# A hybrid block on one Trainium2 core: a Silu on a column of ones as ScalarE's first instruction

## The chip, the core and the metric

The kernel runs on one core of a Trainium2 chip. A core has five engines with an instruction queue each: TensorE (PE; its weight loads are shown apart as PEld), VectorE (DVE), ScalarE (ACT), GpSimd (POOL) and SyncE (SP), which here only issues transfers. The metric is the device time of one launch in microseconds (us). The kernel before took 261.08 us, the median of three runs (260.71 to 262.23).

## The reference

Two blocks follow each other on a sequence of 2048 tokens with 640 channels, in bf16. The first is a convolution block of the H3 kind on a layer-normed input, the second a SwiGLU feed-forward block with 1728 inner columns:

```
h  = x + q' * (conv(kv, ssm_k) + kv * ssm_D)     q' = layernorm(x),  kv = shift_conv(k, 4 taps) * v
h2 = h + (silu(n @ w_gate) * (n @ w_up)) @ w_down     n = layernorm(h)
```

The long convolution is a causal one over all 2048 tokens, written in the reference with an FFT of length 4096.

## The kernel before

The sequence is cut into four blocks of 512 tokens, with 128 partitions of four tokens each. For each block the kernel makes `kv` (a four-tap convolution as small matmuls on transposed k, line 507), takes a short real transform of `kv` and of the filter by matmuls with a cosine and sine table (`WF`, line 317), multiplies spectra on VectorE (lines 552, 553, 578), transforms back (`WI`, line 747), gates and adds, normalizes again and transposes. The feed-forward part of block j runs while the convolution part of block j + 1 is worked on: gate and up products (line 835, and line 870 for the odd columns), Silu on ScalarE (line 852), the up product copied out of PSUM by ScalarE (line 859), their product on VectorE (lines 858 and 861), and the down product (line 902), which is added into the output.

Nothing is scheduled while the program runs or by a compiler. Each step is added with `plan.add` and gets a number in the order of adding; the table `ORDER` lists these numbers in the order in which the steps are emitted, and a negative number picks the step's other engine. A step is a function that may issue several instructions. Each engine works through its own instructions in that order and waits for others by semaphores. PSUM is four buffers `ps` of two banks; a product can only start when the buffer's last reader is done. Large operands share twelve SBUF buffers `big`.

[...] What this kernel asks of ScalarE is Copy (with and without a scale), Identity, Square and Silu. ScalarE's first step is an eviction of transposed k (line 488), a copy; the first Silu is that of line 852 in the feed-forward part of block 0, at some 51 us.

The step which the change touches is that of line 922. It is emitted among the first: a memset of the 128x128 tile `ident` by VectorE, which a select on GpSimd (line 923) then turns into the identity matrix, with which TensorE transposes k (line 486) and runs a few warming matmuls (line 936).

```
dve(100, lambda: nc.vector.memset(ap(ident), 1.0), [], [ident])
plan.add("pool", 700, lambda: nc.gpsimd.affine_select(ap(ident), ap(ident), ...), [], [ident])
```

Of the kernel before, what the change touches and what calls it, by code (L numbers as in the profile page):

```python
# [10 lines left out]
FP32 = mybir.dt.float32  # L11
BF16 = mybir.dt.bfloat16
I32 = mybir.dt.int32
ACT = mybir.ActivationFunctionType
# [5 lines left out]
P = 128  # L20
# [153 lines left out]
def kernel(ctx: ExitStack, tc: tile.TileContext, A_q, A_k, A_v, A_shift_k, A_ssm_k, A_ssm_D, B_x,  # L174
          B_w_gate, B_w_up, B_w_down, out):
    nc = tc.nc
# [23 lines left out]
    def fixed(shp, dt, name):  # L200
        return Buf(None, None, const.tile(shp, dt, name=name))

    def ap(b):
        if b.pool is None:
            return b.ap
        t = place[b.pool][b.at]
        _, how, sizes = views.get(b.kind, (None, None, None))
        return t.rearrange(how, **sizes) if how else t
# [15 lines left out]
    def dve(ns, fn, r, w):  # L224
        return plan.add("dve", ns, fn, r, w)
# [26 lines left out]
    ident = fixed([P, P], BF16, "ident")  # L252
# [666 lines left out]
                     [], [(o, k)])  # L919


    dve(100, lambda: nc.vector.memset(ap(ident), 1.0), [], [ident])
    plan.add("pool", 700, lambda: nc.gpsimd.affine_select(ap(ident), ap(ident), [[-1, P]], ALU.is_equal, 0.0, base=0, channel_multiplier=1), [], [ident])

    def blank():
# [127 lines left out]
```

## Time and profile before

| what | value |
| --- | --- |
| median of three runs | 261.08 us |
| lowest and highest | 260.71, 262.23 us |
| the profiled execution's own time | 260.93 us |
| its span, first to last instruction | 259.1 us |
| granted TensorE clock | 1.00 |
| TensorE, VectorE, ScalarE busy | 248.4, 206.6, 180.1 us |
| ScalarE table loads | 2, of 1283 ns each |

A profile line of a group reads: line of the code, engine, operation, what it writes and reads with the shape, number of instructions; then busy time in us and the mean of one in ns; then the engine's idle time just before them and which instruction ended it. A time line reads: start, length, engine, line, operation, operands, and in brackets the idle time before and its releaser. The chain is the sequence of work that ended last, followed back from the end of the program.

### The profile page before, as it was taken

Reading aid. Unit: us, or ns where it says so; the run is one execution under the profiler, and the core shown is the slowest. Engines: PE = TensorE matmul, PEld = TensorE weight load, DVE = VectorE, ACT = ScalarE, POOL = GpSimd, SP = SyncE. Lnnn points to the kernel's source line nnn. Section 1 sums busy time; section 2 is a strip of 40 time slices with the busy share of each in tenths; the row PEclk is TensorE's granted clock in tenths of the full one; section 3 lists DMA queues with packets and bytes.
Section 4 is the critical chain, followed back from the end, with each engine's and each line's share of the span. In section 5 each row is a group of like instructions: output and inputs, shape, how many; then the busy total and the mean of one; then the engine's idle time right before and its main releaser. Section 6 shows DMA issues by size and latency. Waiting matters only on the chain.

```text
span 259.1 us, 5062 instructions
## 1 busy us (share of the span) xinstructions
PE 248.4 (96%) x2012; PEld 145.1 (56%) x2027; DVE 206.6 (80%) x297; ACT 180.1 (69%) x308; POOL 16.6 (6%) x26
## 2 busy tenths in 40 slices
PE   6799988989999999999999999999999999999995
PEld 3566656444545677654445577544447764444663
DVE  1779999979999999999999999999999821121222
ACT  3399989998999999969969978742553662342300
POOL 2000000000000011020002201400001003000000
PEclk9999999999999999999999999999999999999999
DMA  6999997499569798699491415997699406000011
GB/s 195 353 147 307 272 160 193 106 242 274 111 206 310 129 266 184 118 203 273 123 215 25 78 51 97 220 285 211 176 245 242 100 3 76 0 3 0 0 53 51
DMA packets 73379, 40.82 MB, mean 158 GB/s; under 512 B 33606, under 2 KB 71180, under 8 KB 73356
## 3 DMA queue, kind: packets, MB, share of 16 engines
q1 hardware_dynamic: 71052, 37.88, 59.3%
q0 software_dynamic: 2304, 2.62, 7.0%
q8 instruction: 16, 0.26, 0.4%
q14 instruction: 7, 0.06, 0.1%
HBM read 30.01 MB, written 4.59 MB: 133 GB/s over the span
## 4 chain that ended last, share of the span: by engine, by line
PE 76%; DVE 9%; ACT 7%; DMA 4%; issue 2%; SPq 1%; DVEq 0%; ACTq 0%
PE ps L835 38%; PE ps L902 22%; PE ps L317 7%; PE ps L870 5%; DMA big<-in_A_q_dram 4%; PE ps L747 3%; DVE S L578 2%; ACT S L303 1%; DVE row L760 1%; DVE big L578 1%; DVE bn L677 1%; ACT big L535 1%; ACT big L303 1%; DVE S L352 1%; PE ps L507 1%
## 5 line engine op out<-in xcount | busy, mean ns | idle before, releaser
L835 PE MATMUL ps<-big,big 128*128 128x512 bf16 x469 | 105.3, 379 | 1.5 <-ACT sg L852 0.9
L835 PEld LDWEIGHTS <-big 128*128 128x128 bf16 x480 | 46.8, 98 | 56.2 <-issue 1.6
L902 PE MATMUL ps<-wd,tT 128*128 128x320 bf16 (+2 forms) x447 | 63.6, 299 | 0.4 <-ACT big L535 0.4
L902 PEld LDWEIGHTS <-tT 128*128 128x128 bf16 x448 | 43.2, 98 | 18.4 <-issue 0.4
L852 ACT ACTIVATE sg<-ps 128x1024 bf16<-128x1024 f32 (+1 forms) x28 | 27.0, 964 | 38.1 <-PE ps L835 18.6
L317 PE MATMUL ps<-big,WF 128*128 128x320 bf16 x240 | 39.3, 299 | 1.5 <-ACT S L303 0.5
L552 DVE TENSOR_TENSOR big<-S,S 128x2560 bf16<-128x2560 bf16 x24 | 35.1, 1485 | 0.1
L553 DVE TENSOR_TENSOR S<-S,big 128x2560 bf16<-128x2560 bf16 x24 | 34.9, 1485 | 0.0
L317 PEld LDWEIGHTS <-WF 128*128 128x128 bf16 x240 | 23.1, 97 | 14.0 <-issue 3.1
L861 DVE TENSOR_TENSOR tT<-sg,sg 128x1024 bf16<-128x1024 bf16 (+1 forms) x22 | 14.6, 664 | 13.1 <-ACT sg L859 13.1
L692 ACT ACTIVATE row<-big,sm 128x640 bf16<-128x640 bf16 x23 | 21.0, 928 | 2.7 <-DVE sm L643 2.7
L620 ACT ACTIVATE row<-big 128x640 bf16<-128x640 bf16 x28 | 20.7, 745 | 2.6 <-DVE big L771 2.1
L859 ACT CAST sg<-ps 128x1024 bf16<-128x1024 f32 (+1 forms) x22 | 21.4, 972 | 1.3 <-PE ps L835 1.2
L303 ACT CAST S<-ps 128x320 bf16<-128x320 f32 (+1 forms) x41 | 20.2, 553 | 2.5 <-PE ps L317 2.3
L908 POOL DMA_DIRECT2D out_dram<-row x12 | 10.7, 1052 | 105.2 <-ACT row L907 105.2
L303 ACT ACTIVATE big<-ps 128x640 bf16<-128x640 f32 (+1 forms) x27 | 16.3, 645 | 0.5 <-PE ps L317 0.3
L858 DVE TENSOR_TENSOR tT<-sg,ps 128x1024 bf16<-128x1024 bf16 (+1 forms) x6 | 6.3, 1042 | 13.1 <-PE ps L835 10.6
L747 PE MATMUL ps<-S,WI 128*128 128x320 bf16 x96 | 15.2, 299 | 0.2 <-DVE S L578 0.2
L663 ACT ACTIVATE row<-big 128x640 bf16<-128x640 bf16 x20 | 15.0, 759 | 0.2 <-DMA big<-row 0.2
L870 PE MATMUL ps<-big,big 128*128 128x512 bf16 x57 | 13.8, 379 | 0.1
L747 PEld LDWEIGHTS <-WI 128*128 128x128 bf16 x112 | 10.6, 98 | 5.8 <-issue 0.6
L578 DVE TENSOR_TENSOR big<-S,S 128x2560 bf16<-128x2560 bf16 (+1 forms) x10 | 12.2, 1222 | 0.1
(90 smaller groups left out, 231.5 us busy)
## 6 DMA issues: line engine op xcount, KB each, us to landing
big<-in_B_w_gate_dram SPq DMA_DIRECT2D x24, 320.0 KB, 5.0
big<-in_B_w_up_dram SPq DMA_DIRECT2D x24, 320.0 KB, 4.6
big<-in_A_v_dram SPq DMA_DIRECT2D x4, 640.0 KB, 5.8
big<-in_A_ssm_k_dram SPq DMA_DIRECT2D x4, 640.0 KB, 8.6
big<-in_A_q_dram SPq DMA_DIRECT2D x4, 640.0 KB, 5.8
wd<-in_B_w_down_dram SPq DMA_DIRECT2D x1, 2080.0 KB, 10.7
out_dram<-big SPq DMA_DIRECT2D x3, 640.0 KB, 5.1
out_dram<-row POOLq DMA_DIRECT2D x12, 160.0 KB, 5.0
```

What stands on the lines that cost most here:

```text
L303: (lambda: nc.scalar.activation(dst(), src(), ACT.Copy, scale=2.0)) if twice else (lambda: nc.scalar.copy(dst(), src())),
L317: nc.tensor.matmul(ap(ps)[:, h, 0:NH], w, ap(src)[:, r, h * NH:(h + 1) * NH], start=(first and i == 0), stop=(last and i == len(rs) - 1), ...
L552: dve(1490, lambda b=b, xs=xs, hs=hs: v.tensor_mul(flat2(b), X.part(xs), H.part(hs)), [X.at(xs), H.at(hs)], [b])
L553: dve(1490, lambda b=b, dst=dst, f=f: f(A.part(dst), A.part(dst), flat2(b)), [b], [A.at(dst)])
L620: act(930, lambda r=r, junk=junk: nc.scalar.activation(ap(junk), ap(x)[:, r, :], ACT.Square, scale=D ** -0.5, accum_out=sm(s, 1)[:, r:r + ...
L692: nc.scalar.activation(ap(row), ap(x)[:, r, :], ACT.Identity, bias=sm(s, 5)[:, r:r + 1], scale=sm(s, 4)[:, r:r + 1])
L747: nc.tensor.matmul(ap(ps)[:, w, 0:NH], m, src[:, w * NH:(w + 1) * NH], start=(i == 0), stop=(i == len(terms) - 1))
L835: nc.tensor.matmul(of(ps, i), ap(w)[:, k, off:off + P], ap(hT)[:, k, lo:lo + n], start=(k == 0), stop=(k == KT - 1))
L852: act(1010 if wide else 600, lambda: nc.scalar.activation(of(sg), of(*gate), ACT.Silu), [gate[0]] if gate[0] is up[0] else [(gate[0], gate ...
L859: op = plan.add("act", 1010 if wide else 590, lambda: nc.scalar.copy(of(co), of(*up)), psu + [sg], [co] + tt, ("dve", 1230 if wide else 69 ...
L870: nc.tensor.matmul(ap(ps)[:, i, :], ap(w)[:, k, off:off + P], ap(hT)[:, k, :], start=(k == 0), stop=(k == KT - 1))
L902: nc.tensor.matmul(ap(to)[:, hf, 0:n], ap(tT)[:, c, at:at + P], ap(wd)[:, c, d0:d0 + n], start=(c == order[0]), stop=(c == order[-1]))
```

## The change

The step of line 922 issues three instructions where it issued one: the memset of `ident`, a memset of a new tile `one` of 128 partitions and one column in fp32, and a Silu by ScalarE on that column, in place. Nothing reads `one` afterwards. Both new instructions lie in the same step, so the numbers of the steps and the table `ORDER` stay as they were.

```
-    dve(100, lambda: nc.vector.memset(ap(ident), 1.0), [], [ident])
+    one = fixed([P, 1], FP32, "one")
+
+    def first():
+        nc.vector.memset(ap(ident), 1.0)
+        nc.vector.memset(ap(one), 1.0)
+        nc.scalar.activation(ap(one), ap(one), ACT.Silu)
+    dve(100, first, [], [ident])
```

## The prediction

> **What bounds the kernel now.** I read the page's busy times first, then the ScalarE groups with shapes kept apart, then the chain that ended last around the second table load, then TensorE's waits, and last the time line of all engines around 50 us and of ScalarE and SyncE at the start. The page:
>
> ```profile
> span 259.1 us, 5062 instructions
> ...
> PE 248.4 (96%) x2012; PEld 145.1 (56%) x2027; DVE 206.6 (80%) x297; ACT 180.1 (69%) x308; POOL 16.6 (6%) x26
> ```
>
> TensorE is idle for 259.1 - 248.4 = 10.7 us of the span. That is the whole pot from which an edit that adds and removes no matmul can draw. The ScalarE groups hold two table loads, one at the head of the program and one under the line of the Silu:
>
> ```profile
> L488 ACT ACT_TABLE_LOAD x1 | 1.3, 1283 | 0.8 <-PEq L1037 0.8
> L852 ACT ACT_TABLE_LOAD x1 | 1.3, 1283 | 0.0
> ```
>
> The second stands on the chain that ended last (start, length, what):
>
> ```profile
> 49.34 0.72 ACT row L663 x2
> 50.07 1.28 ACT L852
> 51.36 1.03 ACT sg L852
> 52.40 0.04 issue
> 52.44 4.91 PE ps L835 x22
> ```
>
> ScalarE runs without a gap before it, so the load takes 1.28 us of a queue that is full, and the first Silu (51.36 to 52.38) frees the PSUM buffer that TensorE's next gate or up product needs. From 52 us on TensorE is followed nearly without a break, and its waits there are two:
>
> ```profile
> PE ps L835 <- ACT sg L852: 0.9, 1, 0.9
> PE ps L902 <- ACT big L535: 0.4, 1, 0.4
> ```
>
> The time line of all engines shows who else the load holds up:
>
> ```profile
> 47.71 3.83 PE L835 MATMUL ps<-big,big 128*128 128x512 bf16 x17
> ...
> 50.07 1.28 ACT L852 ACT_TABLE_LOAD   x1
> ...
> 52.44 5.77 PE L835 MATMUL ps<-big,big 128*128 128x512 bf16 x25 [0.90 <-ACT sg L852]
> ...
> 54.44 0.99 ACT L859 CAST sg<-ps 128x1024 bf16<-128x1024 f32 x1
> ...
> 55.47 0.69 DVE L861 TENSOR_TENSOR tT<-sg,sg 128x1024 bf16<-128x1024 bf16 x1 [1.39 <-ACT sg L859]
> ```
>
> TensorE loses 0.90 us and VectorE 1.39 us, both behind ScalarE. At the head of the kernel:
>
> ```profile
> 0.82 1.28 ACT L488 ACT_TABLE_LOAD   x1 [0.82 <-PEq L1037]
> ...
> 0.99 0.17 DVE L922 MEMSET ident<- 128x128 bf16 x1
> ...
> 1.99 0.29 POOL L923 TENSOR_SCALAR_AFFINE_SELECT ident<-ident 128x128 bf16<-128x128 bf16 x1
> ...
> 2.31 0.19 DVE L948 TENSOR_TENSOR eye<-ident 128x64 bf16<-128x64 bf16 x1 [1.16 <-POOL ident L923]
> ...
> 5.47 1.88 ACT L488 COPY kT<-ps 128x640 bf16<-128x640 bf16 x3 [3.37 <-PE ps L486]
> ```
>
> **The change, part by part.** *Removed: the second load.* After it, the copies, squares and Identity passes of lines 303, 620, 663, 692 and 859 go on to the end with no third load, so the set that holds Silu serves all that this kernel asks of ScalarE. If that set is loaded first, nothing calls for another: one load of 1.283 us is gone at 50.07.
>
> *Added on VectorE: a memset of 128 ones.* The nearest row is the memset of line 495, 0.07 us; that of line 922 with 128 columns took 0.17. I take 0.07. It stands at 1.16 us, where VectorE then waits 1.16 us for GpSimd, so it lies in that wait. GpSimd's select needs the memset of ident, done at 1.16, and starts at 1.99 behind GpSimd's own memset (1.39 + 0.52 = 1.91). Even if it waited for both memsets (1.23) nothing would move. Without that cover it would cost 0.07.
>
> *Added on ScalarE: a Silu of one column.* No row has this shape. From below: 0.206, the mean of the 128x1 accumulator reads of line 620. From above: 0.587, the shortest Silu of line 852 (512 columns). I take 0.25, nearer to the one column. The load ahead of it either starts at 0.82 as now, or waits for the memset and runs 1.25 to 2.53. So the Silu ends between 2.3 and 3.2 us. Queued behind it is the copy of line 488, which waits for TensorE until 5.47: 2.3 to 3.2 us of cover. Cost nothing; if the cover were gone, 0.25 plus the 0.4 by which the load may slide.
>
> *Moved: nothing else.* The three new instructions lie in one step of the order table, so the numbers of all steps stay; no DMA issue is passed or moved, on SyncE's queue or GpSimd's.
>
> *What the removed load is worth.* ScalarE gains 1.28 us from 50.07 on, if its next instructions have their inputs. The first Silu reads a gate product, the cast of line 859 at 54.44 the up product after it, whose last matmul ended at 50.48. Even a Silu that had to wait for that one would start at 50.53, 0.83 earlier than now. TensorE can't gain more than its own stall. By the waits it is 0.90. By matmul starts it is a little more: the last matmul before the stall ends at 51.54, and at 0.379 us each it began at 51.16; in an undisturbed stretch one starts every 0.216 us, so the next could have begun at 51.38 and not at 52.44: 1.06. VectorE's wait of 1.39 goes almost wholly (1.28). That matters, since VectorE has next to no idle time from there to 80 us (29.85 of 31.26 us busy between 52.44 and 83.70, the 1.39 being all the rest) and would otherwise hold TensorE at the old pace.
>
> *What is late next.* Transfers. SyncE's run of issues from 50.49 to 57.5 hangs on TensorE at 50.48, before the stall, and does not move. What it brings has room: a gate load issued at 50.88 landed at 55.87 and is first read by TensorE at 58.9; the x block landed at 54.75 and is first read at 58.66; the transposes landed at 59.08 and are read at 65.2. So the least room is 3.0 us, against a shift of 1. The tightest place is VectorE at 62.9, where it passes waits on transfers whose last landing was the output store's, 62.28, if it needs that one: with the store up to 0.14 earlier (it was released by VectorE's line 643 at 57.72, when SyncE had been ready since 57.55), VectorE would keep about 62.9 - 62.28 + 0.14 = 0.76, say 0.8, of its 1.28. The later issues (71.79 behind TensorE's line 317, and so on) move with the engines that release them.
>
> The sum: 0.8 if VectorE is held at 62.9, 1.06 if nothing holds; I take 0.9, the stall as the waits count it. Lower bound of the gain: nothing, if a later wait eats it. Upper bound: 1.06 plus the 0.38 of line 902 at 89.5, where ScalarE's evictions are late: 1.44. The profiled execution took 260.93 (span 259.1 and 1.8 around it) and becomes 260.0; it lies 0.15 under the median of the runs, 261.08, so against that median: 261.08 - 0.9 = 260.2. That is 0.34%, inside the 0.5% that a measurement of this kernel can tell from no change.
>
> **The rivals.** *The gain is given back (chance 0.19).* ScalarE, VectorE and TensorE are all within 2% of full between 84 and 112 us (ScalarE 21.92 of 22.48, VectorE 22.03, TensorE 22.48), and ScalarE's evictions release TensorE there within 0.05 us of need, so a transfer of that stretch that keeps its old time (DMA share 1.01 between 83.7 and 89.5) would hold all three. For it: no slack in any engine. Against it: those transfers are issued after waits on TensorE and ScalarE, and shift too. Time: 260.8 to 261.1.
>
> *More than the stall comes out (0.12).* VectorE and ScalarE get 1.28 where TensorE gets 1.06, so the small late evictions after 61 us and the 0.38 at 89.5 could go as well. Against it: ScalarE at 83.70 itself waits 0.25 for TensorE, so it can't arrive there with more than TensorE's shift. Time: 261.08 - 1.44 = 259.6, which is 0.55% faster.
>
> *Two loads remain (0.03).* If whatever places the loads put them otherwise, the Silu at the head would bring its set and the next copy another, and the load at 50.07 would stay. For it: now the first copy at the head did bring a set without Silu. Against it: a set that serves the next function is kept, as the long run after 51.36 with Silu and copies mixed shows. Time: 261.1, for the second load at the head still ends by 4.5 us, before 5.47. [...]
>
> *Slower: the transfers of 56 to 62 us collide (0.08).* With ScalarE and VectorE 1.28 earlier, the output store of 640 KB is not held any more by line 643 and goes out with the transposes, the k load and the gate load, in a stretch where the DMA share was already 1.68 (56 to 58 us). If that delays what TensorE reads next, the stall comes back larger. It decides only when a landing slips by more than 3.0 - 1.06 = 1.9 us; to be slower by 0.5% (1.3 us) it must slip by 1.9 + 1.06 + 1.3 = 4.3. Against it: the store moves by 0.14 at most. Time: 262.4 to 262.8 if it happens.
>
> **How the numbers follow.** The forecast has 0.58: 260.2, its own range 259.7 to 260.9. The runs of before spread from 260.71 to 262.23, so a median of a few runs can sit 0.3 to 0.5 off. The range for 8 in 10 goes from 259.4, which takes in the larger gain, to 261.5, which takes in the gain lost and an uneven run; left out are the collision and the tails. Faster by over 0.5% means under 259.77: the larger gain, 0.12, and about one in ten of the forecast's own spread, 0.06: 0.18. Slower by over 0.5% means over 262.4: the collision, 0.08. Same: 0.74.
>
> **What would show it.** In the profile after: one table load, with a Silu of 128x1 behind it before 3.3 us, and the copies of line 488 still at about 5.5; no load near 50 us and the first Silu of the gate at about 50.1; no wait of TensorE on it near 51.4; line 861's first product at about 54.2 and not 55.47; the rest of the time line 0.8 to 1.1 us earlier up to the end, with a span of 258.0 to 258.3. The prediction is wrong if TensorE's idle time after 52 us grows by what it lost at 52.4, above all at 62 to 90 us, or if a second load stands at 5 us.

## The result, and the profile after

The changed kernel took 259.81 us (median of 22 runs) where the kernel before, run beside it, took 261.02 (22 runs): a ratio of 0.9953 with a 95% interval of 0.9937 to 0.9968. That is 1.21 us less, where 0.9 was forecast, and the time lies inside the forecast's own range. By its interval the gain is 0.8 to 1.6 us, so the time alone does not tell 1.21 from 0.9; what is finer than that below rests on the traces. The profiled execution took 259.64 us with a span of 257.8 (before: 260.93 and 259.1). The page of the changed kernel:

```profile
span 257.8 us, 5063 instructions
...
PE 248.2 (96%) x2012; PEld 145.4 (56%) x2027; DVE 206.8 (80%) x298; ACT 178.7 (69%) x308; POOL 17.6 (7%) x26
```

TensorE is now idle for 257.8 - 248.2 = 9.6 us and not 10.7; ScalarE is busy for 1.4 us less, of which the load without the new Silu makes 1.28 - 0.20 = 1.08. Among ScalarE's groups with shapes kept apart there is one load where there were two, and the new Silu:

```profile
L927 ACT ACT_TABLE_LOAD x1 | 1.3, 1283 | 0.8 <-PEq L1043 0.8
L927 ACT ACTIVATE one<-one 128x1 f32<-128x1 f32 x1 | 0.2, 203 | 0.0
```

The time line of the start (start, length, what) shows where the new instructions lie:

```profile
0.82 1.28 ACT L927 ACT_TABLE_LOAD   x1 [0.82 <-PEq L1043]
...
1.10 0.06 DVE L926 MEMSET one<- 128x1 f32 x1
...
1.99 0.29 POOL L929 TENSOR_SCALAR_AFFINE_SELECT ident<-ident 128x128 bf16<-128x128 bf16 x1
2.11 0.20 ACT L927 ACTIVATE one<-one 128x1 f32<-128x1 f32 x1
2.31 0.19 DVE L954 TENSOR_TENSOR eye<-ident 128x64 bf16<-128x64 bf16 x1 [1.15 <-POOL ident L929]
...
5.64 0.69 ACT L488 COPY kT<-ps 128x640 bf16<-128x640 bf16 x1 [3.33 <-PE ps L486]
```

The load starts at 0.82 as before: it did not wait for the memset that its Silu waits for. GpSimd's select is still at 1.99. The memset lies in VectorE's wait for it, and the Silu ends at 2.31, 3.33 us before ScalarE's next instruction has its input. That this is at 5.64 and not at 5.47 is not the Silu's doing: among the runs below it is 5.64 without a Silu at the head (the second load in idle time) and 5.45 with it (the shorter delay). Around 50 us the time line of all engines now reads:

```profile
47.32 8.80 PE L835 MATMUL ps<-big,big 128*128 128x512 bf16 x40
...
49.65 0.22 ACT L663 ACTIVATION_READ_ACCUMULATOR row<-big 128x1 f32 x1
49.74 1.04 ACT L852 ACTIVATE sg<-ps 128x1024 bf16<-128x1024 f32 x1
...
52.81 1.03 ACT L859 CAST sg<-ps 128x1024 bf16<-128x1024 f32 x1
...
53.87 0.69 DVE L861 TENSOR_TENSOR tT<-sg,sg 128x1024 bf16<-128x1024 bf16 x1
```

The Silu follows line 663 without a load between, 1.62 us earlier than before (49.74 against 51.36), TensorE runs through, and line 861 has no wait any more. Of the 1.62, 0.17 was there ahead of this place already (see below); the other 1.45 is more than the load's 1.28. Now the Silu starts 0.09 us after the start of the accumulator read ahead of it and overlaps it (49.65 and 49.74). In the kernel before, that read lay here:

```profile
49.83 0.22 ACT L663 ACTIVATION_READ_ACCUMULATOR row<-big 128x1 f32 x1
```

and the load began only when it was over, at 50.07. So the load took some 1.45 us of a full queue and not 1.28. TensorE's waits on other engines from 49 us to the end are down to one:

```profile
PE ps L902 <- ACT big L535: 0.5, 1, 0.5
```

**Where the 1.3 us came from.** Pair the instructions of the two traces, engine by engine in their order, and take the difference of their starts: that gives a shift along the span. TensorE's is -0.17 at 43 to 51 us, -1.23 from the stall on, -1.34 from 61 us, -1.48 from 69 to 166 us, -1.39 from there and -1.28 from 184 us to the end. VectorE's and ScalarE's are -0.17 to -0.18 ahead of 50 us, some -1.6 at 55 us, -1.47 to -1.49 at 81 us and -1.28 at the end. So the step at 50 us is worth 1.31 us for all three engines, some 0.2 of it is given back late, and 0.17 was there ahead of the change's reach.

The 1.31 is more than TensorE's stall of 1.06. The other part is two stalls that no list of waits showed. TensorE's own time line, of the kernel before:

```profile
59.77 1.46 PE L835 MATMUL ps<-big,big 128*128 128x512 bf16 x6
61.19 0.70 PE L317 MATMUL ps<-big,WF 128*128 128x320 bf16 x4
...
67.67 1.79 PE L317 MATMUL ps<-big,WF 128*128 128x320 bf16 x12
69.44 1.24 PE L870 MATMUL ps<-big,big 128*128 128x512 bf16 x5
```

and the same place of the changed kernel:

```profile
58.76 1.24 PE L835 MATMUL ps<-big,big 128*128 128x512 bf16 x5
59.84 0.71 PE L317 MATMUL ps<-big,WF 128*128 128x320 bf16 x4
...
66.32 1.79 PE L317 MATMUL ps<-big,WF 128*128 128x320 bf16 x12
67.95 1.24 PE L870 MATMUL ps<-big,big 128*128 128x512 bf16 x5
```

Look at the starts alone. Twelve matmuls of line 317 and then line 870: 69.44 - 67.67 = 1.77 before, 67.95 - 66.32 = 1.63 after, 0.14 less for the same twelve. At 61.19 matmul by matmul: the last of line 835 starts at 60.85, and the next start is 0.334 us later where 0.216 is the pace, 0.12 too many. Neither line carries a bracket with idle time, because in the time line the end of a matmul lies behind the next start, so behind 512 columns a delay under about 0.16 us (0.379 - 0.216) leaves no gap, nor does one behind the 320 columns of line 317 (0.30 long, 0.136 apart). 1.06 + 0.12 + 0.14 = 1.32.

### The profile page after: what moved, and what is told of

Same layout as the page of the kernel before. It is cut to its first block, busy times and chain, and to the rows that moved or that the text cites. A ratio compares the mean times of both kernels' runs of the same rounds, so it can differ in the third digit from the quotient of the medians.

```text
span 257.8 us, 5063 instructions
## 1 busy us (share of the span) xinstructions
PE 248.2 (96%) x2012; PEld 145.4 (56%) x2027; DVE 206.8 (80%) x298; ACT 178.7 (69%) x308; POOL 17.6 (7%) x26
## 4 chain that ended last, share of the span: by engine, by line
PE 85%; DVE 7%; ACT 5%; issue 2%; POOL 0%; ACTq 0%; DVEq 0%; POOLq 0%
PE ps L835 40%; PE ps L902 23%; PE ps L317 10%; PE ps L870 5%; PE ps L747 3%; DVE S L578 2%; PE ps L507 1%; DVE big L578 1%; ACT S L303 1%; PE ps L942 1%; ACT big L535 1%; DVE big L537 1%; ACT big L303 1%; PE ps L793 1%; ACT row L620 1%
## 5 line engine op out<-in xcount | busy, mean ns | idle before, releaser
L317 PE MATMUL ps<-big,WF 128*128 128x320 bf16 x240 | 39.1, 299 | 1.6 <-ACT S L303 0.8
L317 PEld LDWEIGHTS <-WF 128*128 128x128 bf16 x240 | 23.2, 97 | 13.7 <-issue 3.1
L303 ACT CAST S<-ps 128x320 bf16<-128x320 f32 (+1 forms) x41 | 20.2, 554 | 2.3 <-PE ps L317 2.1
L303 ACT ACTIVATE big<-ps 128x640 bf16<-128x640 f32 (+1 forms) x27 | 16.3, 646 | 0.3
```

The source lines that it names most:

```text
L303: (lambda: nc.scalar.activation(dst(), src(), ACT.Copy, scale=2.0)) if twice else (lambda: nc.scalar.copy(dst(), src())),
L317: nc.tensor.matmul(ap(ps)[:, h, 0:NH], w, ap(src)[:, r, h * NH:(h + 1) * NH], start=(first and i == 0), stop=(last and i == len(rs) - 1), ...
```

## The experiments

"Step" below is the change of that shift between 43 to 50 us and 70 to 100 us, against the trace of the kernel before. It leaves out what differs at the head: there, at 43 us, the profiled executions of these kernels lie between 0.54 us early and 1.94 us late, whatever was edited.

**The same start with another function.** The only edit against the changed kernel is the function:

```
-        nc.scalar.activation(ap(one), ap(one), ACT.Silu)
+        nc.scalar.activation(ap(one), ap(one), ACT.Copy)
```

> The changed kernel with the Silu on the column of ones replaced by a Copy on it: the tile, the memset and ScalarE's extra instruction stay, but the first set loaded is again one without Silu, so the second load stands again ahead of the first gate Silu. Theory (the gain is the stall behind the second load and nothing else): two loads, TensorE waits 0.9 us at about 52.4 again, time that of the kernel before within 0.3 us, ratio 0.999 to 1.001. Rival A (the head of the kernel, the new tile's place in memory or the extra instruction gave part of the gain): 0.2 to 0.6 us faster than before, ratio 0.998 or less, with the stall in place.

Measured: 260.83 us, ratio 1.000 (0.9981 to 1.0019), step 0.00. Its time line around 50 us:

```profile
49.59 1.28 ACT L852 ACT_TABLE_LOAD   x1
50.88 1.02 ACT L852 ACTIVATE sg<-ps 128x1024 bf16<-128x1024 f32 x1
...
51.96 4.26 PE L835 MATMUL ps<-big,big 128*128 128x512 bf16 x19 [0.89 <-ACT sg L852]
```

The second load is back and with it the stall. The tile, the memset and one more instruction at the head are worth nothing by themselves: it is the function that counts.

**The same without the new tile.** The column is one of a tile that is written later anyway (`diag`):

```
-        nc.vector.memset(ap(one), 1.0)
-        nc.scalar.activation(ap(one), ap(one), ACT.Silu)
+        nc.vector.memset(ap(diag)[:, 0, 0:1], 1.0)
+        nc.scalar.activation(ap(diag)[:, 0, 0:1], ap(diag)[:, 0, 0:1], ACT.Silu)
```

> The changed kernel with the Silu on one column of the tile diag, which is written anew later, and no new tile, so that every tile lies in memory where it lay before. Theory: as the changed kernel, ratio to before 0.9953 within 0.0015 and one load. Rival A, memory part: less gain, ratio 0.997 to 1.000.

Measured: 259.45 us, ratio 0.9949 (0.9927 to 0.9972), step -1.31. The profiled execution has a long span, 259.8, since it was 1.94 us late at 43 us already; behind 50 us it gains as the others do. The place of the new tile plays no part.

**Both loads kept, the second one in idle time.** The Silu on the column stands ahead of ScalarE's first copy of line 399 instead of at the head:

```
-        nc.scalar.activation(ap(one), ap(one), ACT.Silu)          # at the head
...
+            def turned_out(copy, r=r, pt=pt):                     # the eviction at line 399
+                if early and copy == nc.scalar.copy:
+                    early.pop()
+                    nc.scalar.activation(ap(one), ap(one), ACT.Silu)
+                copy(ap(gT)[:, r, :], turned(pt)[:, 0:D])
...
```

> The Silu on the column of ones is not ScalarE's first instruction but stands just ahead of block 0's first copy of line 399, at about 8 us, where ScalarE idles for 3.5 to 3.9 us. Two loads, as in the kernel before, but the second hidden. Theory (what costs is where the load stands, not how many there are): as the changed kernel, ratio 0.9953 within 0.0015; the second load at about 7.5 us, copy of line 399 not later than before. Rival B (each load costs its 1.3 us, wherever it stands): as before, 0.999 to 1.001.

Measured: 259.54 us, ratio 0.9956 (0.9935 to 0.9977), step -1.31. ScalarE's time line:

```profile
7.54 1.28 ACT L404 ACT_TABLE_LOAD   x1
8.84 0.20 ACT L404 ACTIVATE one<-one 128x1 f32<-128x1 f32 x1
11.07 0.69 ACT L405 COPY big<-ps 128x640 bf16<-128x640 bf16 x1 [2.03 <-PE ps L399]
```

Two loads, and the whole gain. So the number of loads has no price here; what was paid for was the place of the second, in a queue without a gap.

**The changed kernel once more**, without an edit.

> The changed kernel unaltered, for a second profile on the same chip as the three above. Theory: ratio 0.9953 within 0.0015; TensorE's starts after 72 us 1.2 to 1.5 us earlier than in the first profile of before, and those up to 12 us shifted by whatever the first loads land late, in either direction, up to 0.5 us: the 0.17 us by which the first profile of after was early ahead of the stall is no part of the change. Rival A: the same 0.17 us early at 44 to 50 us again.

Measured: 259.66 us, ratio 0.9943 (0.9921 to 0.9966), step -1.31. At 43 us it lies 0.18 us later than the kernel before, where the first profile of the changed kernel lay 0.17 earlier. The head's 0.17 is therefore no part of the change's effect. It gives back 0.34 us between 150 and 184 us, more than the 0.19 of the first profile.

**Two more loads ahead of the first Silu.** An Exp on the column, at the place where the load had stood, brings a load, and the Silu behind it another (51.15 and 52.66 us in the trace of this run):

```
+            def silu(c=c, j=plan.block):
+                if j == 0 and c == 0:
+                    nc.scalar.activation(ap(one), ap(one), ACT.Exp)
+                nc.scalar.activation(of(sg), of(*gate), ACT.Silu)
...
```

> The changed kernel with an Exp on the column of ones just ahead of the first gate Silu of block 0, where the kernel before had its second load. Exp needs another set, so two loads of 1.28 us and an instruction of 0.2 us come in there: some 2.75 us. Theory as it now stands (ScalarE's queue is the bound from about 44 us to about 88 us, so its time there counts one for one): steps from 50 us on 2.7 to 2.8 us later than in the changed kernel, time about 262.4, ratio to before 1.0055. Rival C (only TensorE's own stall counts: it has about 0.4 us of slack there in the changed kernel and later waits soak up more): 2.0 to 2.35 later, ratio 1.003 to 1.004.

Measured: 263.74 us, ratio 1.0103 (1.0062 to 1.0145), step +2.92 against the kernel before, so 4.23 against the changed one. That is some 1.5 us more than the 2.75 which the loads and the Exp should take. TensorE's time line and the table of engines by stretches of 2 us (granted clock behind POOL) tell why:

```profile
55.03 7.24 PE L836 MATMUL ps<-big,big 128*128 128x512 bf16 x25 [2.39 <-ACT sg L856]
```

```profile
54.00:56.00 2.00, 0.97 (x4) 0.44 (x4) 1.17 (x1) 2.00 (x4) 0.00 (x0) 0.89 1.04 355
56.00:58.00 2.00, 2.00 (x6) 0.70 (x5) 0.00 (x0) 2.00 (x6) 0.00 (x0) 0.50 1.30 255
58.00:60.00 2.00, 2.00 (x9) 0.79 (x8) 1.94 (x3) 1.76 (x4) 0.00 (x0) 0.75 0.78 156
```

The stall itself is 2.55 us between matmul starts, 1.49 more than before. Behind it the granted clock fell to 0.50, and matmuls that start every 0.216 us began up to 0.427 apart from 55.46 to 59.09 us: 1.68 us more. The sum, 1.49 + 1.68, less the 0.26 of the two late stalls, which don't occur in this run, is 2.91. What the expectation had left out is that a stall can cost more than its length, as this one did by 1.68 us. The last runs below look for the length at which it does.

**Two more loads where ScalarE is idle.** The same Exp ahead of the sixth Silu of the last block (`j == NB - 1 and c == 4`), where ScalarE waits 4.68 us:

> The changed kernel with the same Exp and its two loads ahead of the sixth Silu of the last block, at about 232 us, where ScalarE idles for 4.7 us and waits for VectorE's line 858. Theory: 2.75 us fit into 4.7, that Silu still starts as soon as VectorE releases it, no change: ratio to before 0.9953 within 0.0015. Rival B (each load costs its time): 2.6 to 2.8 us slower than the changed kernel, ratio 1.005.

Measured: 260.66 us, ratio 0.9979 (0.9954 to 1.0004). This didn't go as expected:

```profile
233.51 1.28 ACT L855 ACT_TABLE_LOAD   x1
234.80 0.20 ACT L855 ACTIVATE one<-one 128x1 f32<-128x1 f32 x1
238.15 1.28 ACT L856 ACT_TABLE_LOAD   x1 [3.15 <-DVE tT L863]
239.44 1.02 ACT L856 ACTIVATE sg<-ps 128x1024 bf16<-128x1024 f32 x1
```

The first load went into the idle time; the second did not, though 3.15 us of it were left. It starts only when VectorE's line 863 has released the Silu behind it, so the Silu comes 1.3 us late. In this trace TensorE loses 0.17 us by it at 242 us and the end comes 0.18 later; the median lies 0.85 above that of the changed kernel, but the two intervals overlap, so what it costs in the time stays unclear.

**Both loads behind each other in that idle time.** With a Silu of the column behind the Exp, the second load belongs to an instruction that waits for nothing:

```
                 if j == NB - 1 and c == 4:
                     nc.scalar.activation(ap(one), ap(one), ACT.Exp)
+                    nc.scalar.activation(ap(one), ap(one), ACT.Silu)
```

> The changed kernel with two more table loads, both ahead of the sixth Silu of the last block and both behind each other without a wait of that Silu's between them: load, Exp of one column, load, Silu of one column, about 2 x 1.283 + 2 x 0.2 = 2.97 us, in an idle time of ScalarE of 4.7 us. Theory (a load costs only what stands behind it at that moment): the four end about 1.7 us before the Silu's input is there, the Silu and line 861 do not move, and the time is that of the changed kernel, ratio to before 0.995 within 0.0015. Rival (a load costs its 1.28 us wherever it stands, or each drains the engine for more): ratio 0.9995 to 1.005.

Measured: 259.69 us, ratio 0.9934 (0.9911 to 0.9958), step -1.31.

```profile
232.44 1.28 ACT L855 ACT_TABLE_LOAD   x1
233.74 0.20 ACT L855 ACTIVATE one<-one 128x1 f32<-128x1 f32 x1
233.96 1.28 ACT L856 ACT_TABLE_LOAD   x1
235.25 0.20 ACT L856 ACTIVATE one<-one 128x1 f32<-128x1 f32 x1
237.10 1.02 ACT L857 ACTIVATE sg<-ps 128x1024 bf16<-128x1024 f32 x1 [1.65 <-DVE tT L864]
```

Three loads in the program, and the time of one. The Silu at 237.10 still waits 1.65 us for VectorE, and it lies where it lay in the changed kernel, 0.27 later, as everything is in this execution from 220 us on. Of a cost beyond the load's own time and that of the function behind it nothing is seen: the four instructions start 1.30, 0.22 and 1.29 us apart, where a load takes 1.28 and a function of one column 0.20. In the full queue at 50 us the load took 1.45 us in all.

**The wait that is left.** The one wait of TensorE after 49 us, at 88 us, is for ScalarE's evictions of line 535. One exchange in the order table puts one eviction earlier:

```
-    ... 312, 466, 467, 315, 314, 469,
+    ... 312, 466, 467, 315, 469, 314,
```

> The changed kernel with two neighbours of ScalarE's queue swapped: the eviction of line 535 at 87.4 us, for which TensorE waits 0.3 to 0.5 us at 88 us, goes ahead of the normalizing pass of line 692 at 86.6 us. Rival C (TensorE's own stalls are what counts): 0.3 to 0.5 us faster than the changed kernel, TensorE's wait at 88 us gone, ratio to before about 0.994. Theory (ScalarE's queue is the bound there, and a swap leaves its sum as it is): the wait at 88 us gone or smaller, but given back within 25 us, no gain over 0.15 us, ratio 0.9953 within 0.0015.

Measured: 259.31 us, ratio 0.9960 (0.9929 to 0.9991), step -1.30. The wait at line 902 is gone, and in its place line 317 starts 0.37 us late at 92.41 (the list of waits says 0.2, `PE ps L317 <- ACT big L303`). The shift of ScalarE and VectorE is -1.84 both ahead of that stretch and behind it, so what was won was returned within 5 us. The shorter profiled span, 257.3, comes from its head, which was 0.54 us early. There is no faster version in this.

**A shorter delay in the same place.** A copy of 128x512 into a tile that nothing reads, ahead of the first Silu of the changed kernel:

```
+                if j == 0 and c == 0:
+                    nc.scalar.copy(ap(pad).rearrange("p (a b) -> p a b", a=4), same(4))
...
```

> The changed kernel with a copy of 128x512 in bf16 by ScalarE into an unused tile, about 0.6 us, just ahead of the first gate Silu: half of what a load takes there. Theory: one for one, steps from 55 us on 0.5 to 0.6 us later against those at 44 us, ratio to before 0.9975. Rival C: TensorE has about 0.4 us of slack there, so 0.1 to 0.2 later at 98 us, ratio 0.996.

Measured: 259.77 us, ratio 0.9963 (0.9944 to 0.9982), step -0.90: 0.41 us were lost, less than the 0.5 to 0.6 that were expected. This loss stands in the trace; the ratio alone does not tell this run from the changed kernel.

```profile
49.72 0.64 ACT L856 COPY pad<-ident 128x512 bf16<-128x512 bf16 x1
50.23 1.05 ACT L857 ACTIVATE sg<-ps 128x1024 bf16<-128x1024 f32 x1
```

The Silu was delayed by 0.51 (50.23 - 49.72), and TensorE's starts show three stalls: 0.15 at 51.33, 0.12 at 60.08 and 0.13 at 68.32, together 0.40. Two of them are those that the change had removed at 61.19 and 69.44. This is the clearest evidence that they belong to the same late queue of ScalarE. The changed kernel has only about 0.1 us to spare there (0.51 - 0.41).

**Longer stalls without a further load.** The last three runs start with the Copy at the head, so that the load stands at 50 us as it did before the change, and put one, two or three of these copies ahead of it.

> The first activation is a Copy, so the second table load stands at about 50 us as before the change, and one copy of 128x512 into an unused tile (pitch 0.51 us) stands ahead of the first gate Silu. TensorE's stall should be 1.06 + 0.51 = 1.57 us between matmul starts. Theory 1 (a stall only costs its length): matmuls after it start 0.216 us apart as ever, the step against the kernel before is +0.5 us. Theory 2 (a stall of more than about one us also lowers TensorE's granted clock for the next microseconds, as after the 2.55 us stall of two loads): a dip of the granted clock below 0.9 between 54 and 60 us and a step above 0.8 us. I expect theory 1 here: about 261.5 us.

> As the run with one copy, with two copies of 128x512 ahead of the first gate Silu: a stall of 1.06 + 1.02 = 2.08 us. Theory 1 (length only): step +1.0 us against the kernel before, granted clock full behind it, about 262.0 us. Theory 2 (the clock falls after a long stall): granted clock about 0.5 over some 2 us behind the stall, matmuls 0.43 us apart, step +1.0 + 1.5 = 2.5 us, about 263.5 us. Open between them: 2.08 lies between the stall of 1.06 that had no such tail and that of 2.55 that had one.

> Three copies of 128x512 ahead of the first gate Silu: a stall of 1.06 + 1.53 = 2.6 us, as long as that of the two loads but with one load less. Theory 2 (length of the idle time decides): the granted clock falls to about 0.5 for some 2 us behind it and the step is +1.5 + 1.5 = 3.0 us against the kernel before, about 264 us. Theory 1 with the loads as the cause of the tail: clock full, step +1.5 us, about 262.5 us.

The second and third copy took 0.65 us each of the queue and not 0.51, so the stalls came out a little longer than planned. By matmul starts, with the two loads of above put in (stall, wait, clock and step are those of the profiled execution, the kernel before is counted as run beside the copies; the last column counts all executions whose mean clock was 0.993 or 0.994, where the others had 0.999 or 1.000):

| ahead of the first Silu | stall by starts, us | wait in the list, us | lowest clock | step, us | ratio | executions with a low mean clock |
| --- | --- | --- | --- | --- | --- | --- |
| load (the kernel before) | 1.06 | 0.90 | 1.00 | 0 | 1 | 0 of 24 |
| one copy, load | 1.57 | 1.40 | 1.00 | +0.50 | 1.0013 (0.999 to 1.0036) | 0 of 8 |
| two copies, load | 2.21 | 2.05 | 1.00 | +1.14 | 1.0043 (1.0017 to 1.0069) | 1 of 8 |
| load, Exp, load | 2.55 | 2.39 | 0.50 | +2.92 | 1.0103 (1.0062 to 1.0145) | 4 of 6 |
| three copies, load | 2.86 | 2.70 | 0.50 | +3.22 | 1.0118 (1.008 to 1.0156) | 2 of 2 |

The table by stretches, of two copies:

```profile
54.00:56.00 2.00, 1.69 (x8) 0.78 (x8) 0.79 (x1) 2.00 (x6) 0.00 (x0) 1.00 1.07 322
56.00:58.00 2.00, 2.00 (x11) 0.91 (x10) 0.66 (x2) 2.00 (x5) 0.00 (x0) 1.00 1.28 217
```

and of three:

```profile
54.00:56.00 2.00, 0.89 (x4) 0.37 (x4) 0.95 (x1) 1.99 (x5) 0.00 (x0) 0.89 1.04 322
56.00:58.00 2.00, 2.00 (x6) 0.68 (x5) 0.00 (x0) 2.00 (x5) 0.00 (x0) 0.50 1.20 212
58.00:60.00 2.00, 2.00 (x8) 0.84 (x7) 1.86 (x3) 1.68 (x4) 0.00 (x0) 0.75 0.87 193
```

In the traces with up to 2.05 us of idle time a stall costs its length: 1.57 - 1.06 = 0.51 and 2.21 - 1.06 = 1.15 are the steps of +0.50 and +1.14. At 2.39 and 2.70 the clock falls as well, with one load in the queue as with two, so it is the idle time that does it and not the loads. (With three copies the longer stall, 1.80, and the slow matmuls, 1.68, less the 0.26 of the two late stalls that are gone, make the step of 3.22.) There is no sharp bound in it. The means of 0.89, 0.50 and 0.75 over the three stretches, with the full clock on either side, are 0.44 + 2.00 + 1.00 = 3.44 us at half clock in each of these two traces; that lowers the mean of an execution of some 263 us by 0.0065, and by that mean the clock also fell in one of the eight executions with two copies and stayed full in two of the six with two loads. Both busy times read 2.00 at 56 to 58 us; only the count (x6 against x11) and the clock show that half the work was done.

## Why the prediction was right, and where it was off

**The second load goes: right.** One load is left, at 0.82, and no other follows for any function of the kernel: what it brought in (its set) serves them all. The rival in which two remain would have had no gain. The run with the Copy first is that case: it has two loads, though the changed kernel does with one, and no gain. In these traces a set stays until a function calls for another: with the Copy first the second load stands at 49.59, ahead of the first Silu, with the Silu first there is none after 0.82, and an Exp at 50 us brings two.

**Memset 0.07, Silu 0.25, both at no cost: right.** They took 0.06 and 0.20. Of the two ways the load could go it went the better one: it did not wait for the memset. The cover of 2.3 to 3.2 us was 3.33.

**"TensorE can't gain more than its own stall": this step failed, by 0.26 us.** The stall of 1.06, which the prediction had worked out from matmul starts, went entirely. But the delayed queue of ScalarE released TensorE late at two more places, by 0.12 at 61.19 and 0.14 at 69.44. There the list of waits and the time line show no idle time. The prediction had set 0.9 by the waits against 1.06 by the starts for the stall that was visible, and then didn't look along the starts for others. Besides, it took the smaller of these two as its term. The term should have read 1.32 in place of 0.9. That the total still came out close is in part luck: this term was 0.42 too small, and the sum had nothing for the up to 0.34 us that are given back later.

**"ScalarE gains 1.28": it gained 1.45.** The load had also cost the overlap of the Silu with the instruction ahead of it. TensorE could not use all of that: ScalarE's shift, less the 0.17 of the head, is 1.46 at 55 us and 1.31 from 62 us on, which TensorE's reaches at 69 us.

**"VectorE at 62.9 might keep 0.8 of 1.28": it did not bind.** Line 578, which stands behind the waits of 62.9, starts at 61.75 in place of 63.23, so VectorE keeps 1.31 there (1.48 less 0.17). The output store, which was taken as a bound and thought to go out up to 0.14 earlier, went out at 58.0 in place of 57.58 and landed at 62.3: line 578 did not wait for it.

**The rival "more than the stall comes out" (259.6) was half right.** Its small late evictions after 61 us did go, and they are 0.26 of the 0.42 by which the step is larger than 0.9; the rest is the stall by starts in place of by waits. Its other half, the wait of line 902 at 88 us, did not go: it is 0.5 instead of 0.4, because ScalarE and TensorE arrive there with the same shift. The prediction had named that reason against it. The run with the exchanged eviction shows that even without this wait nothing is won.

**The rival "given back" happens, in another place and in part.** It was looked for between 84 and 112 us, where the shift is flat at -1.48. (The busy times of 22.48 us that the prediction gives for that stretch are those of 89.52 to 112; over the whole of it they are 27.44 to 27.62 of 28.00, which says the same.) What comes back, 0.19 us in the first profile, comes between 150 and 184 us. The waits of ScalarE from 145 to 166 us hold the line that changed; before:

```profile
ACT row L663 <- DMA big<-row: 0.2, 1, 0.2
```

and after:

```profile
ACT row L663 <- DMA big<-row: 0.5, 1, 0.5
```

ScalarE's line 663 waits for transfers of GpSimd's queue. The last of them was issued 1.47 us earlier, as the engines were (143.73 against 145.20), but landed only 1.09 earlier (146.91 against 148.00), and ScalarE's shift there is -1.09. SyncE's transposes behind it (line 786) go out 1.28 earlier and not 1.47, and so does the gate load behind them. Before, it landed at 167.03, TensorE loaded the first weights from it at 167.08, and their matmul started at 167.29, at the usual pace. After, it landed at 165.85, the weights were loaded at 165.89, and the matmul started at 165.90, 0.08 later than the pace would have had it. TensorE's weight loads have a wait there that the kernel before hasn't:

```profile
PEld L835 <- DMA big<-in_B_w_gate_dram: 0.4, 1, 0.4
```

The other 0.11 TensorE loses at 183 us, where it comes to the -1.28 that VectorE has had since 152 us. The prediction's "least room is 3.0 us" was looked up between 50 and 65 us only; this transfer, 100 us later, had 0.05 to its weight load. In the other profiles with the step at 50 us, the waits of 0.6 went with 0.34 given back, of 0.2 and 0.3 with 0 to 0.12, and no wait with none. That order fits, and in the second profile of the changed kernel the same transfer landed 0.59 earlier (147.41), with ScalarE's shift there at -0.59. But no run changed this transfer by itself, and why it took longer when it was issued earlier (3.18 and 3.36 us in place of 2.80) stays open; so this cause is read from the traces and not tested.

**The sum.** 1.31 from the step, less 0 to 0.34 given back, is 0.97 to 1.31 in the profiles; the medians show 1.21. The rival of a collision of transfers between 56 and 62 us did not occur: there is no wait of TensorE in that stretch.

## What to carry to other kernels

In these runs a table load cost what stood behind it in ScalarE's queue at that moment: 1.31 us where the queue was full, nothing at the head or in an idle stretch, with two loads as with three. In the idle stretch behind 232 us the second load was hidden only where the instruction that it belongs to had nothing to wait for (load at 233.96); with the late Exp alone it came behind its Silu's wait (238.15). One function set served this kernel, and a dummy Silu at the very start brought it in for 0.20 us of idle time; with a Copy there the second load stayed at 49.59. When you price a stall, go through the starts of the matmuls for as long as the late engine stays without slack, since small stalls behind it, 0.12 and 0.14 us here, need not show as idle time; and look for the tightest landing over the whole kernel, not only next to the edit.

## What the hardware showed beside that

**TensorE's clock after a stall.** In the traces, idle times of 0.90, 1.40 and 2.05 us left the granted clock at 1.00. After those of 2.39 and 2.70 us it reads 0.89 from 54 to 56 us, 0.50 from 56 to 58 and 0.75 from 58 to 60, in both: some 3.4 us at half clock, if it was full on either side (0.44 + 2.00 + 1.00). TensorE had resumed shortly before, at 55.03 and 55.11. That phase, with 512 columns every 0.427 us in place of 0.216, costs 1.68 us on top of the stall. Over all executions the share with a low mean clock grows with the stall: none of eight at 1.57 us, one of eight at 2.21, four of six at 2.55 and both at 2.86. What tells the executions of one kernel apart is not shown, since those without a trace have only their mean clock, and so this stays open.

**Where a load stands against a wait.** At the head the load ran ahead of what its instruction waits for: at 0.82 both in the kernel before, where the copy behind it had its input at 5.47, and in the changed one, where the memset was done at 1.16. In the run with the late Exp the load at 238.15 came only after the Silu's wait of 3.15 us. Why the one goes ahead and the other doesn't was not tried; in the run that put a free Silu of the column in front, the load had no such wait and hid entirely.
